# One load for wo and one for w1, two more w2 blocks as column products, and a bf16 turn of the result

## The chip, the cores and the metric

The kernel runs on one core of one Trainium2 chip. The metric is the device time of an execution in microseconds (us); each time below is the median of several executions, with the range. A profile shows a slightly shorter *span*, from the first to the last instruction: in most executions here 1.3 us less than the time. All executions named below count as fast: none is more than 1.5% above the fastest of the same kernel. The engines are PE (tensor; PEld is its weight load), DVE (vector), ACT (scalar), POOL (GpSimd) and SP, whose queue issues all loads. Sixteen DMA engines carry the data.

## The reference

One decode step of a conditioned transformer block, two sequences, one new token each. Cut to what matters:

```python
mod = (silu(c) @ w_mod)                       # six shift, scale and gate vectors
h = layernorm(x) * (1 + ca) + sa
q = h @ wq                                    # 32 heads of 128
p = softmax(q @ k_cache.T / sqrt(128))        # 4 kv heads, 32768 keys: 8 pairs (batch, kv head)
x = x + ga * ((p @ v_cache) @ wo)             # wo: 4096 x 1024, 8.4 MB
h = layernorm(x) * (1 + cb) + sb
z = gelu(layernorm(h) @ w1 + b1)              # w1: 1024 x 3584, 7.3 MB
x = x + gb * (z @ w2 + b2)                    # w2: 3584 x 1024, 7.3 MB
```

Two rows of work against 178 MB of weights and cache: the kernel mostly reads.

## The kernel before

All loads go through one ring of 160 KB per partition, in a fixed order: w_mod, wq, then for each of the eight pairs two K halves (slots at 0 and 32 KB) and V (slot at 64 KB), then wo, w1, w2. A load is issued as soon as what lay in its place has been used; `frees` makes the queue wait for that.

```python
for m, off in enumerate((128, 0)):
    add(("wo", m), [16, DM], A_wo[m * 2048:(m + 1) * 2048, :].rearrange("(p j) n -> p j n", j=16), off * KB)
for m, off in enumerate((32, 64)):
    add(("w1", m), [4, F], w1_v[:, 4 * m:4 * m + 4, :], off * KB)
W2_ITEMS = ((0, 8, 96), (8, 16, 112), (16, 24, 128), (24, 27, 144), (27, 28, 150))   # blocks j0..j1 at KB
```

The output layers come in two shapes. A *row product* holds the activations still (128x32) and streams 512 weight columns past them; four of them fill the four column groups of the array, and the sums lie in rows that must be turned into columns afterwards (`load_row`, a DVE copy, then `to_columns`, four products with a small selection matrix). A *column product* holds 128x128 weights still and streams two activations; its sums are columns at once.

```python
for m in range(2):                       # wo: 2 x 32 row products into one bank
    it = need("wo", m)
    for j in range(16):
        for hf in range(2):
            ...matmul(psS[0][32 * q:32 * q + 32, :], lhsT=atT[m][:, j, :], rhs=w[:, j, hf * 512:(hf + 1) * 512])
load_row("dve", psS[0], "psS0", 0)
to_columns(psM, "psM", 0, True, True)
# ... residual, two layernorms, then w1: 8 x 8 row products, transpose, gelu -> gT ...
for g in range(16):                      # w2, first 16 blocks: row products
    ...
load_row("dve", psS[0], "psS0", 3)
to_columns(psO, "psO", 3, True, False)
for g in range(16, FT):                  # w2, last 12 blocks: 8 column products each, added on top
    ...
mT = psO * mod(5); res_bf = mT + x1b     # two DVE operations
matmul(psM[0:16, 0:128], lhsT=res_bf, rhs=ident)     # turn to 16 rows of 128, fp32 PSUM
res16 = copy(psM[0:16, 0:128])
```

## Time and profile before

| | |
|---|---|
| time | 420.07 us, 3 executions, 420.02 to 420.12 |
| span of the profiled execution | 418.7 us |
| DMA queue busy, share of the span | 98.8% |
| PE, DVE, ACT busy | 70%, 50%, 36% |
| bytes read from HBM | 178.28 MB, 426 GB/s over the span |

Two lines of the page: from part 1 the busy time of each engine, and from part 6 the issue of wo (count, size of each, median us from issue to landing).

```profile
PE 291.0 (70%) x5183; PEld 231.3 (55%) x5183; DVE 209.6 (50%) x423; ACT 149.4 (36%) x179; POOL 6.8 (2%) x29
...
wo<-in_A_wo_dram SPq DMA_DIRECT2D x2, 4096.0 KB, 39.0
```

No compute engine is busy for the whole span. A 4 MB load takes about 9.7 us by itself at 430 GB/s but lands 39 us after its issue: some 30 us of other loads stand ahead of it. That backlog is what a change of issue times eats into.

### The profile page before, as it was taken

To read this page: it belongs to the slowest core of one execution; us is meant where nothing else is said; L and a number is where in the kernel's file an instruction comes from. 1 tells how busy PE (TensorE), PEld (TensorE's weight loads), DVE (VectorE), ACT (ScalarE), POOL (GpSimd) and SP (SyncE) were. 2 spreads that over 40 slices of the span, in tenths; PEclk is the share of its full clock that TensorE was granted. 3 is DMA by queue.
4 is the path that set the end of the run, shared out by engine and by line. 5 is a ranking of instruction groups with operands and counts; after the bars stand their busy time and mean duration, and the time that the engine had idled before them with its cause. 6 is when DMAs were issued, how large, how long until landed. Compare 5 with 4: busy or idle time off the path is not lost.

```text
span 418.7 us, 11609 instructions
## 1 busy us (share of the span) xinstructions
PE 291.0 (70%) x5183; PEld 231.3 (55%) x5183; DVE 209.6 (50%) x423; ACT 149.4 (36%) x179; POOL 6.8 (2%) x29
## 2 busy tenths in 40 slices
PE   1407449766996895699369957976995699564536
PEld 1104219762993794299149926962894399221214
DVE  1201105546677676467726664766477567620411
ACT  2000015533565364256405632643365166400100
POOL 3000000000000000000000000000000000000000
PEclk9999557986896997799589958986697889576585
DMA  9989999999999999999999999999999999899995
GB/s 373 450 380 449 448 404 493 398 406 446 441 432 429 423 451 429 419 454 457 391 435 476 407 416 448 438 438 426 438 438 426 416 460 457 377 448 428 424 427 249
DMA packets 5581, 178.42 MB, mean 426 GB/s; under 512 B 698, under 2 KB 706, under 8 KB 964
## 3 DMA queue, kind: packets, MB, share of 16 engines
q1 hardware_dynamic: 5572, 178.28, 98.8%
q8 instruction: 8, 0.13, 0.1%
q14 instruction: 1, 0.01, 0.0%
HBM read 178.28 MB, written 0.00 MB: 426 GB/s over the span
## 4 chain that ended last, share of the span: by engine, by line
DMA 71%; PE 24%; DVE 2%; issue 1%; ACT 1%; SPq 1%
DMA V<-in_A_v_cache_dram 39%; DMA wo<-in_A_wo_dram 10%; DMA K<-in_A_k_cache_dram 10%; PE psZ L584 10%; DMA w<-in_B_w_dram 9%; PE psKT L536 8%; DMA wmod<-in_w_mod_dram 4%; PE psS L548 1%; PE psZ L548 1%; PE psS L655 1%; PE psZ L729 1%; PE psZ L469 1%; ACT KT_sb L540 0%; PE psS L469 0%; DVE m1c L553 0%
## 5 line engine op out<-in xcount | busy, mean ns | idle before, releaser
L536 PE MATMUL psKT<-ident,K 128*128 128x128 bf16 x2048 | 163.1, 229 | 11.5 <-DMA K<-in_A_k_cache_dram 11.5
L540 ACT ACTIVATE KT_sb<-psKT 128x1024 bf16<-128x1024 bf16 x96 | 98.2, 1025 | 124.4 <-PE psKT L536 124.4
L542 DVE COPY KT_sb<-psKT 128x1024 bf16<-128x1024 bf16 x160 | 106.7, 688 | 61.6 <-PE psKT L536 61.2
L536 PEld LDWEIGHTS psKT<-ident,K 128*128 128x128 bf16 x2048 | 126.7, 102 | 13.0 <-DMA K<-in_A_k_cache_dram 12.7
L584 PE MATMUL psZ<-V,E_sb 128*32 128x512 bf16 x512 | 46.4, 541 | 23.2 <-DMA V<-in_A_v_cache_dram 20.0
L548 PE MATMUL psS<-qcur,KT_sb 128*128 128x8 bf16 x1024 | 44.7, 167 | 2.2 <-issue 2.2
L584 PEld LDWEIGHTS psZ<-V,E_sb 128*32 128x32 bf16 x512 | 18.7, 130 | 47.7 <-issue 38.8
L548 PE MATMUL psZ<-qcur,KT_sb 128*128 128x8 bf16 x1024 | 43.0, 167 | 2.2 <-issue 1.5
L548 PEld LDWEIGHTS psS<-qcur,KT_sb 128*128 128x128 bf16 x1024 | 40.0, 97 | 2.3 <-issue 2.3
L548 PEld LDWEIGHTS psZ<-qcur,KT_sb 128*128 128x128 bf16 x1024 | 37.9, 96 | 3.4 <-issue 1.6
L572 ACT ACTIVATE E_sb<-S_sb 128x512 bf16<-128x512 f32 x32 | 19.5, 630 | 29.6 <-DVE S_sb L570 29.6
L570 DVE TENSOR_TENSOR S_sb<-S_sb,gmb 128x512 f32<-128x512 f32 x32 | 20.0, 685 | 0.3
L576 DVE TENSOR_REDUCE rs<-E_sb 128x8 f32<-128x512 bf16 x32 | 19.7, 675 | 0.0
L469 PE MATMUL psS<-wmod,inT 128*32 128x512 bf16 x32 | 5.1, 624 | 16.2 <-DMA wmod<-in_w_mod_dram 16.2
L553 DVE TENSOR_REDUCE m1c<-psZ 128x8 f32<-128x512 f32 x16 | 11.1, 693 | 10.2 <-ACT S_sb L552 10.1
L595 DVE RECIPROCAL rinv<-psM 128x1 f32<-128x1 f32 x8 | 1.3, 168 | 27.7 <-PE psM L593 27.7
L605 PE MATMUL psM<-msum,hmat 128*128 128x128 f32 x16 | 4.2, 347 | 13.3 <-DVE msum L600 13.3
L559 PE MATMUL psM<-identf,m 128*8 128x128 f32 x16 | 4.3, 369 | 13.1 <-DVE m L556 13.1
L553 DVE TENSOR_REDUCE m1c<-psS 128x8 f32<-128x512 f32 x16 | 11.1, 693 | 3.2 <-ACT S_sb L552 3.1
L552 ACT ACTIVATE S_sb<-psZ 128x512 f32<-128x512 f32 x16 | 9.5, 595 | 7.5 <-PE psZ L548 7.5
L477 DVE COPY S_sb<-psS 128x512 f32<-128x512 f32 x1 | 0.7, 690 | 22.9 <-PE psS L469 22.9
L469 PEld LDWEIGHTS psS<-wmod,inT 128*32 128x32 bf16 x32 | 1.1, 132 | 19.3 <-DMA wmod<-in_w_mod_dram 18.0
(123 smaller groups left out, 167.5 us busy)
## 6 DMA issues: line engine op xcount, KB each, us to landing
K<-in_A_k_cache_dram SPq DMA_DIRECT2D x16, 4096.0 KB, 27.1
wq<-in_A_wq_dram SPq DMA_DIRECT2D x2, 4096.0 KB, 44.8
wo<-in_A_wo_dram SPq DMA_DIRECT2D x2, 4096.0 KB, 39.0
w<-in_B_w_dram SPq DMA_DIRECT2D x2, 3584.0 KB, 32.5
wmod<-in_w_mod_dram SPq DMA_DIRECT2D x1, 6144.0 KB, 29.8
w<-in_B_w_dram SPq DMA_DIRECT2D x3, 2048.0 KB, 37.8
wmod<-in_w_mod_dram SPq DMA_DIRECT2D x1, 4608.0 KB, 15.8
wmod<-in_w_mod_dram SPq DMA_DIRECT2D x1, 1536.0 KB, 6.0
```

Of the source, the lines that this page charges most:

```text
L469: pe(lambda e, w=it.view, k=k, kk=kk, ch=ch, n=n, q=q: e.matmul(bank[n][32 * q:32 * q + 32, :], lhsT=inT[:, k, :], rhs=w[:, kk, ch * 512:( ...
L536: pe(lambda e, kq=kq, jj=jj, w=kt, t=t: e.transpose(psKT[kq][:, jj * 128:(jj + 1) * 128], w[:, t, :], ident[:, :]), reads=[it.reg, "ident" ...
L540: act(lambda e, src=src: e.activation(KT_sb[g8][:, :, :], src, ACT.Copy), reads=[f"psKT{kq}"], writes=[f"KT_sb{g8}"], sem=f"ev{cc}_{g8}")
L542: dve(lambda e, src=src: e.tensor_copy(KT_sb[g8][:, :, :], src), reads=[f"psKT{kq}"], writes=[f"KT_sb{g8}"], sem=f"ev{cc}_{g8}")
L548: pe(lambda e, t=t, jj=jj: e.matmul(ps[:, t * HPG:(t + 1) * HPG], lhsT=KT_sb[g8][:, jj, :], rhs=qcur[:, :], start=True, stop=True), reads= ...
L552: act(lambda e: e.activation(Sc, ps.rearrange("p (t h) -> p h t", h=HPG), ACT.Copy), reads=[preg], writes=[f"S_sb_{cc}"], sem=f"sc{cc}")
L553: dve(lambda e: e.tensor_reduce(m1c[:, :, cc], ps.rearrange("p (t h) -> p h t", h=HPG), AX.X, ALU.max), reads=[preg], writes=[f"m1c{cc}"])
L559: pe(lambda e: e.matmul(psM[0:HPG, 0:128], lhsT=m1[:, :], rhs=identf[:, :], start=True, stop=True), reads=["m1", "identf"], writes=["psM"])
L570: dve(lambda e: e.tensor_tensor(Sc, Sc, gmb[:, :].unsqueeze(2).to_broadcast([128, HPG, TPC]), ALU.subtract), reads=[f"S_sb_{cc}", "gmb"], ...
L572: act(lambda e: e.activation(Ec, Sc.rearrange("p h (u t) -> p u h t", t=4), ACT.Exp, scale=SCALE), reads=[f"S_sb_{cc}"], writes=[f"E_sb_{c ...
L576: dve(lambda e: e.tensor_reduce(rs4[:, :, cc], Ec.rearrange("p u h t -> p h u t"), AX.XY, ALU.add), reads=[f"E_sb_{cc}"], writes=[f"rs4_{c ...
L584: pe(lambda e, t4=t4, tg=tg, q=q: e.matmul(psO[32 * q:32 * q + 32, :], lhsT=E_sb[:, tg // 4, :, :].rearrange("p h t -> p (h t)"), rhs=vt[: ...
```

## The change

Its intent: fewer and larger loads for the two output layers of the attention and the feed-forward part, less row work just ahead of the last loads, and a cheaper end. Wo becomes one load with 64 KB in a row for each partition, w1 one load with 56 KB. The ring places move accordingly. The attention result is laid out for the new order of wo's rows (other shapes of the same small operations in the loop). Blocks 14 and 15 of w2 go from row to column products and run beside the row copy. The result is turned by a transpose into a bf16 PSUM tile. The core of the diff:

```diff
-W2_ITEMS = ((0, 8, 96), (8, 16, 112), (16, 24, 128), (24, 27, 144), (27, 28, 150))
+W2_ITEMS = ((0, 8, 64), (8, 16, 80), (16, 24, 0), (24, 27, 16), (27, 28, 22))
+W2_ROWS = 14
...
-    for m, off in enumerate((128, 0)):
-        add(("wo", m), [16, DM], A_wo[m * 2048:(m + 1) * 2048, :].rearrange("(p j) n -> p j n", j=16), off * KB)
-    w1_v = B_w1.rearrange("(p k) n -> p k n", k=KT8)
-    for m, off in enumerate((32, 64)):
-        add(("w1", m), [4, F], w1_v[:, 4 * m:4 * m + 4, :], off * KB)
+    add(("wo", 0), [32, DM], A_wo.rearrange("(p j) n -> p j n", j=32), 0)
+    add(("w1", 0), [8, F], B_w1.rearrange("(p k) n -> p k n", k=KT8), 104 * KB)
...
-    for g in range(16):
+    for g in range(W2_ROWS):
...
     load_row("dve", psS[0], "psS0", 3)
-    to_columns(psO, "psO", 3, True, False)
+    for g in range(W2_ROWS, 16):
+        w2_columns(g, g == W2_ROWS)
+    to_columns(psO, "psO", 3, False, False)
...
-    pe(lambda e: e.matmul(psM[0:16, 0:128], lhsT=res_bf..., rhs=ident[:, :], start=True, stop=True), ...)
-    dve(lambda e: e.tensor_copy(res16[:, :], psM[0:16, 0:128]), ...)
+    pe(lambda e: e.transpose(psKT[0][0:16, 0:128], res_bf..., ident[:, :]), ...)
+    dve(lambda e: e.tensor_copy(res16[:, :], psKT[0][0:16, 0:128]), ...)
```

## The prediction

> **What bounds the kernel now.** I read the page first (engine shares, slices, queues), then the chain that ended last in order of time, then the timeline of the last 80 us, because every part of the change acts after 330 us except three loop operations of the same size. From the page:
>
> ```profile
> DMA  9989999999999999999999999999999999899995
> ...
> q1 hardware_dynamic: 5572, 178.28, 98.8%
> ...
> DMA 71%; PE 24%; DVE 2%; issue 1%; ACT 1%; SPq 1%
> ```
>
> The first row is the busy share of the 16 DMA engines in 40 slices: it is full from the second slice to the last but one. The second says that the packets of the load queue fill 98.8% of the span, 0.988 x 418.7 = 413.7 us. So no more than 5 us of the span are free of transfers, and they lie at the two ends: about 2 us until the first load runs, and about 3 us after the last one. The chain (third row) agrees. A change in compute is worth nothing unless it shortens that last stretch. The tail of the chain, as start, length and what:
>
> ```profile
> 330.98 41.08 DMA wo<-in_A_wo_dram
> 372.10 3.28 PE psS L655 x32
> 375.40 37.83 DMA w<-in_B_w_dram
> 413.27 1.87 PE psZ L729 x64
> 415.17 1.03 PE psZ L729 x32
> 416.22 0.19 DVE mT L732
> 416.43 0.24 DVE res_bf L733
> 416.72 0.29 PE psM L734
> 417.03 0.28 DVE c L736
> ```
>
> Read it as one stream of loads that lasts until the third w2 item is in (413.27), then 96 small products back to back, then two vector operations, the turn, a copy and the store. Between 372 and 413 the tensor engine does all of the two output layers inside the waits for loads. The timeline shows how much room is there (start, length, engine, what, and in brackets the idle time and its releaser):
>
> ```profile
> 355.02 21.65 SPq L389 DMA_DIRECT2D w<-in_B_w_dram  x7
> 372.10 3.25 PE L655 MATMUL psS<-wo,atT 128*32 128x512 bf16 x32 [0.78 <-DMA wo<-in_A_wo_dram]
> 381.73 3.55 PE L655 MATMUL psS<-wo,atT 128*32 128x512 bf16 x32 [6.39 <-DMA wo<-in_A_wo_dram]
> 385.34 0.69 DVE L664 COPY S_sb<-psS 128x512 f32<-128x512 f32 x1 [13.23 <-PE psS L655]
> 395.75 1.68 PE L696 MATMUL psZ<-w,inT 128*32 128x448 bf16 x16
> 398.74 1.35 PEld L696 LDWEIGHTS psZ<-w,inT 128*32 128x32 bf16 x32 [0.38 <-DMA w<-in_B_w_dram]
> 400.59 1.12 DVE L704 STREAM_TRANSPOSE S_sb<-psZ 128x896 f32<-128x896 f32 x1 [2.84 <-PE psZ L696]
> 403.68 1.05 PE L720 MATMUL psS<-w,gT 128*32 128x512 bf16 x16 [3.15 <-DMA w<-in_B_w_dram]
> 408.41 1.90 PE L720 MATMUL psS<-w,gT 128*32 128x512 bf16 x16 [3.69 <-DMA w<-in_B_w_dram]
> 411.11 1.87 PE L668 MATMUL psZ<-half,S_sb 128*128 128x4 f32 x8 [0.80 <-DVE S_sb L664]
> ```
>
> The loads' landings can be read off the waits that they end: wo halves 372.1 and 381.7, second half of w1 398.7, w2 items 403.7, 408.4 and 413.27. The row-shaped part of w2 ends at 411.11 + 1.87 = 412.98, only 0.3 us ahead of the landing that it must beat. That 0.3 us is the narrow place.
>
> **What the Trainium skill says.** "DMA: Bandwidth & Descriptors", Specifications, gives 435 GB/s as the ceiling of the path into SBUF. The trace agrees that nothing is left: the second wo half, 4.194 MB, landed 381.73 - 372.10 = 9.63 us after the first, 435 GB/s; w1 and three w2 items, 13.63 MB, took 413.27 - 381.73 = 31.54 us, 432 GB/s. The same page, "Queues, rings and completion order", says each DMA engine consumes its ring's descriptors in order; the trace fits, since landings follow the issue order. So a load that is issued early enough loses nothing by being issued later. "TensorE: Matmul & The Clock Gate", Part 1, gives half clock until about 3.4 us of sustained work. The trace shows it: the first half of wo took 3.25 us at a granted clock near 0.5, about 107 ns a product, while 32 products of w1 after 398.74 took 1.79 us, 56 ns each. "VectorE: DVE Perf Modes", "Why PSUM operands drop a tier", says an fp32 PSUM operand runs at 1x and that 2x_1P is the most any PSUM operand gets. In the trace the fp32 copy of 512 columns took 690 ns and the bf16 copy of 1024 columns 688 ns, so bf16 from PSUM does go twice as fast here.
>
> **The change, part by part.**
>
> Wo in one load, placed at 0 to 64 KB. Before, the first half went to a free slot and was issued at 330.98. Now the load needs both K slots, and the second is free when its last transposes end: 355.02, when the first w1 load is issued today. The queue still holds the last V load then; its products start at 362.51. So 7.5 us of backlog remain, and no gap opens. The w1 load now needs the V slot, free at about 368.8 (products start 362.51 and take 6.34), with wo still running to 381.7: 12.9 us of backlog. The third w2 item waits for wo's products, at worst 388.2 (381.7 + 6.5), with w1 and two w2 items queued until 408.4. No gap either.
>
> Larger packets. The trace's records of single packets (no view prints them) give medians of 1213 ns for 32 KB, 2418 ns for 64 KB and 1062 ns for 28 KB. Wo: 16 engines carry 256 packets of 32 KB, 16 each, 19.41 us; in 64 KB packets 8 x 2.418 = 19.34. That is 0.06 us less. For w1 at 56 KB I take the same relative gain, 0.33% of 17 us, 0.06 us. Two loads fewer save two completions, perhaps 0.03 us. Sum 0.13 to 0.15 us, and it does reach the end: every later landing moves forward.
>
> Later start of wo's products. They now all wait for 381.6. The attention product has the same shape and count, 64 of 128x512, and took 5.2 to 6.5 us by the chain (6.34 in its last round, cold). Starting cold and warming after 3.4 us gives 3.4 + 32 x 0.054 = 5.2; so 386.9 to 388.1, against 385.3 now: 1.6 to 2.8 us later, all of it in compute. From the row copy to the first w1 product today is 395.75 - 385.34 = 10.41 us, so the input of w1 is ready at 397.3 to 398.5. W1's single load lands at 398.6. So the delay vanishes into that wait.
>
> W1 in one load. 64 products of 448 columns start at 398.6, where 32 were done by then before. Cold they take 94 ns (448 columns at the cold rate above), warm about 50 to 56. All cold: 6.0 us, to 404.6; warming after 3.4 us: 36 cold, 28 warm, 4.9 us, to 403.5. Today the transpose starts at 400.59. So this costs 2.9 to 4.0 us. The transpose, gelu and product with it need 403.68 - 400.59 minus the wait, which is 2.15 us (400.59 to 402.74), so w2's input is ready at 405.7 to 406.8.
>
> W2. Its first item landed at 403.6: 16 products of 1.05 to 1.75 us end at 406.8 to 408.5. The second lands at 408.3. Now 12 row products follow instead of 16: 12/16 of about 1.75 + 0.15 us of drain gives 1.45, to 409.8 or 410.0. The row copy of 0.69 us follows, and beside it on the tensor engine run the 16 column products of blocks 14 and 15, 16 x 29 ns = 0.46 us (29 ns from 2.91 us for 96). They are hidden in the copy. Turning the row takes 1.87 cold: 412.4 to 412.6. This is ahead of 413.1, the new landing of the third item; the margin is 0.5 to 0.7 us instead of 0.3. So the two extra column blocks buy 0.4 us in the narrow place, which only serves as room.
>
> The tail. 96 column products as before. The turn of the result stays one instruction of about 0.28 us. Its copy reads 128 columns of bf16 instead of fp32: from 690 ns for 512 fp32 columns and 278 for 128, a column costs 1.07 ns and the fixed part is 140; at half a column's cost it is 140 + 69 = 209. Gain 0.07 us.
>
> Sum: -0.14 in the stream, -0.07 in the tail, the compute delay hidden: 420.07 - 0.21 = 419.86.
>
> **The rivals.** First, the compute chain no longer fits: if wo's and w1's products both fall badly in the clock windows, or a product takes longer with all weights in one stage, the row turn ends after 413.1 and every excess goes to the end one for one. The cold sums put the end at 412.6 at the latest, so I expect at most 0 to 0.8 us of loss, up to 420.7. The 0.3 us of margin today speak for it, the four fewer row products against it. Second, a gap in the load stream: if 7.5 us of backlog at 355 are not enough because the later issue finds engines that drained early, there would be a wait of up to 1 to 2 us before wo. The landings of the attention loop, where V is issued with one or two loads queued ahead and the row of slices stays full, speak against it. It would make 421 to 422. Third, larger packets may do nothing, and only the tail counts: 420.0. Fourth, a warm clock at the end would shorten the 96 column products, but only to the last landing, which is near 415.8; at most 0.2 us, 419.6.
>
> **Range and chances.** Mostly a sum of tenths, so a narrow range: 419.3 if packets and clock both help and the chip is a little faster, 420.7 if the first rival is at work. A change of 2% would need 8.4 us, more than the span that is free of transfers, so faster by 2% can be ruled out: 0.005. Slower by 2% would need a gap that no backlog above allows: 0.015.
>
> **What would show it.** Right: load queue share still near 98.8%; wo's 64 products start near 381.6 and w1's 64 near 398.6, both after a wait for their load; the transpose of w1's sums at 403.5 to 404.6; the row turn ending before the wait for the third w2 item, near 413.1; the final copy near 0.21 us. Wrong: an idle stretch of the DMA row around 343 to 365, a row turn that directly precedes the last column products without a wait for a load, or landings of wo and w1 that moved by more than 0.5 us.

## The result, and the profile after

| | before | changed |
|---|---|---|
| time, same rounds | 420.14 us (420.02 to 420.28, 6 executions) | 420.32 us (419.88 to 421.27, 6 executions) |
| the same again, other rounds | 420.00 us (419.92 to 420.23, 9) | 420.10 us (419.79 to 420.31, 5) |
| span of the profiled execution | 418.7 us | 418.6 us |

The ratio is 1.0006 in the first rounds (95% interval 0.9993 to 1.0019) and 1.0000 in the second (0.9987 to 1.0014). A ratio is the mean time of one kernel's fast runs over that of the other's of the same rounds, so not quite the ratio of the medians quoted. The change made no measurable difference.

The page after, the same three rows as the prediction shows of before: DMA share by slice, load queue, chain by engine.

```profile
DMA  9989999999999999999899999999999999999996
...
q1 hardware_dynamic: 5284, 178.28, 98.8%
...
DMA 65%; PE 32%; DVE 1%; issue 1%; ACT 0%; SPq 0%
```

The queue has 288 packets fewer (5572 - 5284) and is as full as before. The third row looks like a shift from DMA to PE, but it is not one in the stage of the change: the chain only takes another way through the attention loop, where PE's release of a K slot and the load that follows are followed back in turn. The tail of the chain shows what ends the kernel (start, us, what):

```profile
354.93 26.79 DMA wo<-in_A_wo_dram
...
381.76 6.55 PE psS L652 x49
...
388.33 24.90 DMA w<-in_B_w_dram
...
413.27 2.86 PE psZ L716 x96
...
416.65 0.29 PE psKT L736
...
416.96 0.21 DVE c L737
```

Wo is issued at 354.93 instead of 330.98 and 344.68 (its halves), and its last part is in at the same time as before (381.76 against 381.73). The 96 column products start at 413.27 in both kernels, to the hundredth. The last copy took 0.21 us instead of 0.28. Between these, the timeline (start, length, engine, what, and the idle time before with its releaser):

```profile
381.76 6.51 PE L652 MATMUL psS<-wo,atT 128*32 128x512 bf16 x64 [10.67 <-DMA wo<-in_A_wo_dram]
388.33 0.69 DVE L661 COPY S_sb<-psS 128x512 f32<-128x512 f32 x1 [16.45 <-PE psS L652]
398.76 0.17 PEld L693 LDWEIGHTS psZ<-w,inT 128*32 128x32 bf16 x8 [0.73 <-DVE inT L497]
405.07 1.12 DVE L701 STREAM_TRANSPOSE S_sb<-psZ 128x896 f32<-128x896 f32 x1 [4.27 <-PE psZ L693]
407.27 2.60 PE L725 MATMUL psS<-w,gT 128*32 128x512 bf16 x28 [2.26 <-DVE gT L708]
408.40 0.14 PEld L725 LDWEIGHTS psS<-w,gT 128*32 128x32 bf16 x8 [0.58 <-DMA w<-in_B_w_dram]
409.93 0.69 DVE L661 COPY S_sb<-psS 128x512 f32<-128x512 f32 x1 [2.42 <-PE psS L725]
410.68 1.87 PE L665 MATMUL psZ<-half,S_sb 128*128 128x4 f32 x8 [0.28 <-DVE S_sb L661]
413.27 2.85 PE L716 MATMUL psZ<-gT,w 128*128 128x2 bf16 x96 [0.73 <-DMA w<-in_B_w_dram]
```

Read it against the same rows in the prediction. Every compute step up to the row products of w2 is later: wo's row copy 388.33 against 385.34, w1's transpose 405.07 against 400.59, w2's first row products 407.27 against 403.68. The row products of the first w2 item now wait for gT, made by DVE, and no longer for their load. The 2.60 us of the 28 are two stretches: the weight loads of the second item, at 408.40, still waited for theirs, and began when they had before (408.41). So the later start is gone there. The row copy after 12 instead of 16 products of that item starts at 409.93 instead of 410.36, the row turn ends at 410.68 + 1.87 = 412.55 instead of 412.98, and the last row waits 0.73 us for its load.

### The profile page after: what moved, and what is told of

Read it like the earlier page. It is cut to its first block, busy times and chain, and to the rows that moved or that the text cites. A ratio compares the mean times of both kernels' runs of the same rounds, so it can differ in the third digit from the quotient of the medians.

```text
span 418.6 us, 11630 instructions
## 1 busy us (share of the span) xinstructions
PE 294.4 (70%) x5195; PEld 235.5 (56%) x5195; DVE 209.7 (50%) x423; ACT 149.4 (36%) x179; POOL 7.3 (2%) x28
## 3 DMA queue, kind: packets, MB, share of 16 engines
q1 hardware_dynamic: 5284, 178.28, 98.8%
## 4 chain that ended last, share of the span: by engine, by line
DMA 65%; PE 32%; DVE 1%; issue 1%; ACT 0%; SPq 0%
DMA K<-in_A_k_cache_dram 49%; PE psKT L534 21%; DMA wo<-in_A_wo_dram 6%; DMA w<-in_B_w_dram 6%; DMA wmod<-in_w_mod_dram 4%; PE psS L546 4%; PE psZ L546 2%; PE psS L652 2%; PE psZ L582 1%; PE psZ L716 1%; PE psZ L467 1%; PE psS L467 0%; DVE msum L598 0%; DVE m1c L551 0%; DVE KT_sb L540 0%
## 5 line engine op out<-in xcount | busy, mean ns | idle before, releaser
L534 PE MATMUL psKT<-ident,K 128*128 128x128 bf16 x2048 | 165.1, 230 | 11.5 <-DMA K<-in_A_k_cache_dram 11.5
L534 PEld LDWEIGHTS psKT<-ident,K 128*128 128x128 bf16 x2048 | 128.6, 103 | 13.1 <-DMA K<-in_A_k_cache_dram 13.0
L582 PE MATMUL psZ<-V,E_sb 128*32 128x512 bf16 x512 | 46.8, 546 | 23.2 <-DMA V<-in_A_v_cache_dram 21.5
L652 PE MATMUL psS<-wo,atT 128*32 128x512 bf16 x64 | 6.5, 596 | 10.7 <-DMA wo<-in_A_wo_dram 10.7
```

The source lines that it names most:

```text
L534: pe(lambda e, kq=kq, jj=jj, w=kt, t=t: e.transpose(psKT[kq][:, jj * 128:(jj + 1) * 128], w[:, t, :], ident[:, :]), reads=[it.reg, "ident" ...
L582: pe(lambda e, t4=t4, tg=tg, q=q: e.matmul(psO[32 * q:32 * q + 32, :], lhsT=E_sb[:, tg // 4, :, :].rearrange("p h t -> p (h t)"), rhs=vt[: ...
L652: pe(lambda e, w=it.view, j=j, hf=hf, q=q: e.matmul(psS[0][32 * q:32 * q + 32, :], lhsT=atT[:, j, :], rhs=w[:, j, hf * 512:(hf + 1) * 512] ...
```

## The experiments

Theory: the stream of loads sets the end, the whole change lies beside it, and the single loads have used up room in the compute chain. Rivals: compute spills over in some runs; larger packets shorten the stream; the later issue opens a gap.

### Changed kernel again

No edit; on the same chip and in the same rounds as the next three.

> The changed kernel unaltered, to have it on the same chip as the next three. Theory (the load stream sets the end, all compute of the change is hidden): 420.0 us, a ratio to before between 0.999 and 1.001, profiled span 418.6 +- 0.2. Rival (compute after wo no longer fits in some runs, as a 421.27 us run with a span of 420.0 suggests): some runs 0.5 to 1.5 us longer than the shortest, a wider spread than before has.

It gave 420.10 us (419.79 to 420.31), spans of 418.5 to 418.9. The wider spread of the first rounds did not come back. Two of those six executions had 2.0 us outside a normal span of 418.6, and one, of 421.27 us, had a span of 420.0. No trace of that one was kept.

### The w2 part undone

```diff
-W2_ROWS = 14
+W2_ROWS = 16
-        w2_columns(g, g == W2_ROWS)
-    to_columns(psO, "psO", 3, False, False)
+        w2_columns(g, False)
+    to_columns(psO, "psO", 3, True, False)
```

> The changed kernel with the w2 part undone: 16 blocks of w2 as row products again, none more as columns. Theory: the row turn ends about 0.4 us later than in the changed kernel (412.55), near 413.0, still just ahead of the third w2 item (413.27); time the same as the changed kernel within 0.2 us. Rival (the two column blocks are needed to hold the time): the turn ends after 413.3 and the time rises by 0.2 to 0.5 us.

It gave 419.85 us (419.82 to 419.88), ratio 0.9996 (0.9982 to 1.0009). The row turn ended at 412.05, not near 413.0: the turn itself ran at full clock, in 1.05 us instead of 1.87. So 16 row blocks also fit.

> The changed kernel with 16 row blocks again, a second time: the first gave 419.82 to 419.88 where the changed kernel gave 419.79 to 420.31. If undoing the w2 part is worth 0.2 us: 419.8 to 419.9 again with the narrow spread. If that was a good draw: 419.8 to 420.3.

419.97 us (419.88 to 419.98), beside 420.02 of before. Both intervals contain 1 (the second ratio is 0.9997, 0.9983 to 1.001). The two extra column blocks neither pay nor cost anything that these runs can tell.

### Both loads in two again

```diff
-    add(("wo", 0), [32, DM], A_wo.rearrange("(p j) n -> p j n", j=32), 0)
+    for m in range(2):
+        add(("wo", m), [16, DM], wo_v[:, 16 * m:16 * m + 16, :], 32 * m * KB)
-    add(("w1", 0), [8, F], B_w1.rearrange("(p k) n -> p k n", k=KT8), 104 * KB)
+    for m, off in enumerate((104, 132)):
+        add(("w1", m), [4, F], w1_v[:, 4 * m:4 * m + 4, :], off * KB)
```

> The changed kernel with wo and w1 each in two loads again (halves of a partition's 64 and 56 KB), the rest as changed. Theory: same landings within 0.1 us, time the same within 0.2 us; wo's products end near 385.3 instead of 388.3 and w1's sums are turned near 400.6 instead of 405.1, so the compute has 3 to 4 us more room, which the time does not show. Rival (larger packets or fewer loads shorten the stream): 0.1 to 0.2 us slower than the changed kernel and landings later by that. Rival (compute spills in some runs of the changed kernel): narrower spread than the changed kernel, and 0.1 to 0.5 us faster on average.

It gave 421.00 us (420.09 to 421.31), ratio 1.002 (1.0006 to 1.0034), the slowest of its rounds. But its spans were 418.5 to 418.7, as short as the others'. The excess lay outside the profiled span, 1.4 to 2.6 us there instead of 1.3. In the profile the copy of wo's rows started at 385.28 and w1's transpose at 401.82, about 3 us earlier than in the changed kernel; the weight loads of w2's second item stood idle for 3.73 us until it landed, against 0.58 in the changed kernel and 4.18 in the kernel before; and the last products started at 413.43. Is the excess a property of the kernel?

> The changed kernel with wo and w1 in two loads each, a second time: the first gave 420.09 to 421.31 with spans of 418.5 to 418.7, that is, 1.4 to 2.6 us outside the profiled span where other kernels have 1.3. If that belongs to the kernel: 420.6 to 421.3 again in most runs. If it belonged to those executions: 420.0 to 420.3 and 1.3 us outside the span.

420.16 us (419.98 to 420.36), 1.3 to 1.6 us outside the span. So the excess belonged to those executions. What it was stays open. The room moved by 3 us and the end did not, as the theory says, and it is the single loads that take the room. What fewer loads bring, no time shows; the section on why has what the landings show.

### A known delay, in both kernels

Sixty-four further products of wo's shape ahead of the real ones, written to a bank that is overwritten later; the result stays right. In the changed kernel they stand ahead of all of wo, in the kernel before ahead of its second half.

```diff
     it = need("wo", 0)
+    for x in range(64):
+        pe(... matmul(psS[1][32 * (x % 4):32 * (x % 4) + 32, :], lhsT=atT[:, 0, :], rhs=w[:, 0, 0:512], start=True, stop=True) ...)
```

> The changed kernel with 64 further products of the same shape ahead of wo's 64, into a bank that is overwritten later (the result stays right): a known delay of 3 to 4 us in the compute between wo and w2, no more bytes. Theory (the single loads moved the room from before w1 to after w2's rows, and about 0.7 to 1.5 us of it is left): the third w2 item still lands near 413.3, but the row turn ends after it, and the time rises by 1.3 to 3.0 us, to 421.5 to 423. Rival (all compute is hidden with ample room as in the kernel before): no change, 420.0 to 420.3.

> The kernel before with the same 64 further products ahead of the second half of wo, into the same bank. Theory (before, the compute chain waits some 3.7 us for the second w2 item, so a delay upstream is absorbed there): w2's first row products start 3 us later, the time stays within 0.3 us of the kernel before. Rival (the delay adds to the end): 2 to 4 us slower, as in the run before this one.

| | time | before, same rounds | ratio |
|---|---|---|---|
| changed kernel with the delay | 422.12 us (421.63 to 422.17) | 420.10 us | 1.0044 (1.0027 to 1.0060) |
| kernel before with the delay | 420.15 us (420.06 to 420.21) | 420.10 us | 1.0001 (0.9984 to 1.0018) |

The timeline of the changed kernel with the delay, from w1's transpose on:

```profile
408.36 1.12 DVE L706 STREAM_TRANSPOSE S_sb<-psZ 128x896 f32<-128x896 f32 x1 [4.06 <-PE psZ L698]
...
413.99 1.87 PE L670 MATMUL psZ<-half,S_sb 128*128 128x4 f32 x8 [0.27 <-DVE S_sb L666]
415.72 2.70 PE L721 MATMUL psZ<-gT,w 128*128 128x2 bf16 x96
```

And of the kernel before with it:

```profile
405.12 1.12 DVE L710 STREAM_TRANSPOSE S_sb<-psZ 128x896 f32<-128x896 f32 x1 [3.15 <-PE psZ L702]
...
410.40 1.05 PE L674 MATMUL psZ<-half,S_sb 128*128 128x4 f32 x8 [0.80 <-DVE S_sb L670]
413.42 2.87 PE L735 MATMUL psZ<-gT,w 128*128 128x2 bf16 x96 [1.96 <-DMA w<-in_B_w_dram]
```

In the first, the transpose is 3.3 us later than without the delay (408.36 against 405.07), the row turn ends at 415.86, and the column products follow it without any wait for a load. The time rises by 2.0 us. In the second, the transpose is 4.5 us later (405.12 against 400.59), and the column products still wait 1.96 us for their load. This is the main thing that the change did to the kernel, and its time does not show it. Before, compute between wo and w2 could be 4.5 us slower for nothing; now a delay of 3.3 us costs 2.0.

### Wo issued after V has landed

Wo takes V's place in the ring, w1 the K places; the queue then issues wo only when the last attention product is done.

```diff
-    add(("wo", 0), ..., 0)
-    add(("w1", 0), ..., 104 * KB)
+    add(("wo", 0), ..., 64 * KB)
+    add(("w1", 0), ..., 0)
-W2_ITEMS = ((0, 8, 64), (8, 16, 80), (16, 24, 0), (24, 27, 16), (27, 28, 22))
+W2_ITEMS = ((0, 8, 128), (8, 16, 144), (16, 24, 64), (24, 27, 80), (27, 28, 86))
```

> The changed kernel with wo placed on V's slot instead of K's two slots (w1 takes the K slots, w2 the free ones): wo is issued only when the last attention product is done, near 368.5, while the last V load landed at 362.4. Theory (the stream is full only as long as a load is issued before the one ahead has landed; the changed kernel has 7.5 us of that): the DMA engines stand idle from 362.4 to the issue plus about 1.9 us (the first load of the kernel took that from issue to data), 8.0 us, and the time rises by 7.5 to 8.5 us, to 427.5 to 428.5. Rival (the move of the issue is hidden by other transfers or the compute sets the end): under 2 us.

It gave 429.92 us (429.16 to 430.40), ratio 1.0230 (1.0213 to 1.0248). The DMA row of its page and its issue of wo, from the timeline:

```profile
DMA  9999999999999999999999999999999995599895
...
368.80 0.35 SPq L387 DMA_DIRECT2D wo<-in_A_wo_dram  x1
...
390.67 5.84 PE L652 MATMUL psS<-wo,atT 128*32 128x512 bf16 x64 [19.45 <-DMA wo<-in_A_wo_dram]
```

The two fives are the gap. Wo landed at 390.67 instead of 381.76, 8.9 us later, of which 6.4 are the later issue (368.80 against V's landing at 362.4) and 2.5 the way from issue to data (390.67 - 368.80, less eight packets of 2.418 us). I had taken 1.9 for the latter. A further 1.2 us came between wo and the third w2 item, which is told below. So the changed kernel's wait for both K slots is safe only because the last V load is still running then.

### Small packets for wo

```diff
-    add(("wo", 0), [32, DM], A_wo.rearrange("(p j) n -> p j n", j=32), 0)
+    add(("wo", 0), [32, DM], A_wo.rearrange("(j p) n -> p j n", j=32), 0)
```

> The changed kernel with wo's rows dealt to the partitions one by one, so that its load is 4096 packets of 2 KB instead of 128 of 64 KB (the result is wrong on purpose: the rows no longer fit the stationary operand). Theory (the stream costs the sum of its packets' times, 84 ns for 2 KB and 2418 ns for 64 KB, and every microsecond of it reaches the end): 256 x 84 ns = 21.5 us against 19.3, so all later landings and the time move by 2.2 us, to 422.2. Rival (packet overheads are hidden, so that the size of packets does not count, and the 0.13 us that the prediction gave to larger packets is nothing): within 0.3 us of the changed kernel.

It gave 421.45 us (421.00 to 421.77), ratio 1.0033 (1.0016 to 1.0050). Wrong rows meet the stationary operand, as intended; the comparison still passed, so it is not sharp enough to see this part. The load queue of its page, and the wait that wo's landing ended:

```profile
q1 hardware_dynamic: 9252, 178.28, 99.0%
...
382.83 5.20 PE L652 MATMUL psS<-wo,atT 128*32 128x512 bf16 x64 [12.78 <-DMA wo<-in_A_wo_dram]
```

With 3968 packets more (9252 - 5284) wo landed 1.07 us later (382.83 against 381.76), half of the 2.2 expected, and the end moved by about as much: the spans are 419.7 to 419.9, against 418.6 to 419.0 for the kernel before in the same rounds and 418.5 to 418.9 for the changed kernel in others. The median rose by more, 1.35 us, but two of the four executions had 1.9 us outside the span. So whatever lengthens the stream does reach the end. But the records of single packets cannot simply be added: 256 packets of 84 ns per engine are 21.5 us, and the load took about 20.4, the changed kernel's 19.35 plus 1.07. The records of small packets overlap.

### Two attempts to beat both

After the last load there remain column products, two DVE operations, the turn, the copy and the store. In both attempts the residual is turned early into an fp32 PSUM tile (in a wait) and the last product is accumulated on it by its own turn, so that one DVE operation goes.

```diff
+    matmul(psM[0:16, 0:128], lhsT=x1r, rhs=identf, start=True, stop=False)        # early
-    mT = psO * mod(5); res_bf = mT + x1b; transpose(psKT[0][0:16, 0:128], res_bf, ident)
+    mR = psO * mod(5)                                                             # bf16
+    matmul(psM[0:16, 0:128], lhsT=mR, rhs=ident, start=False, stop=True)
```

The first attempt stands on the kernel with both loads in two:

> An attempt to beat both: loads in two as in the run before, and the last addition taken off the end: the residual with its bias term is turned early into the fp32 PSUM tile, and the last product's turn is accumulated on it, so that one vector operation (0.24 us) and its hand-over go, while the last copy reads fp32 again (+0.07 us). Theory (everything after the last load counts one for one): 0.15 to 0.2 us off the stretch from the last column product to the store (1.07 us in the changed kernel), time near 419.8. If the end were bound elsewhere: no difference.

420.09 us (419.79 to 420.26), no gain. The store was issued at 417.04 instead of 417.20, but landed at 418.70. Its instruction queue and its store (size, us from issue to landing), from the page's DMA parts:

```profile
q8 instruction: 9, 0.15, 0.1%
...
out_dram<-c SPq DMA_DIRECT2D x1, 4.0 KB, 1.6
```

Before and after have eight such fetches and 1.4 for the store. The ninth ran at 416.4 for 1.29 us. Of the store's 16 landings, 15 came by 418.39 and one at 418.67. The second attempt stands on the changed kernel's loads and 16 row blocks, with fewer instructions:

> Second attempt to beat both: the changed kernel's single loads, w2 with 16 row blocks again, and the residual accumulated into the turn as in the first attempt. In the first attempt the store was issued 0.14 us earlier than in the changed kernel but landed 1.66 us after its issue instead of 1.41; its trace has a ninth instruction fetch of 16 KB, at 416.4 us and 1.29 us long, beside the store. This version has fewer instructions than the first attempt and about as many as the run with 16 row blocks, which had eight fetches and none there. Theory (the fetch held back the store): eight fetches, store landing 1.2 to 1.4 us after its issue, span 418.3 to 418.4, time 419.7. Rival (the store lands when the stream's last load plus about 2.9 us is over, whatever its issue): span 418.5 to 418.7, as all others.

```profile
q8 instruction: 8, 0.13, 0.1%
...
out_dram<-c SPq DMA_DIRECT2D x1, 4.0 KB, 1.3
```

Eight fetches; all 16 landings of the store between 418.23 and 418.39. The time was 419.86 us (419.59 to 419.99) beside 420.02 of before, ratio 0.9994 (0.9981 to 1.0008); spans 418.3 to 418.7. It holds the lowest single time, 419.59, and the profiled stretch is shorter as predicted. But the interval contains 1, so it is not shown to be faster.

### More instruction fetches

Semaphore increments that nobody waits for, 400 to 700 to an engine, ahead of wq's products and of the attention loop.

```diff
+    for _ in range(700):
+        T.raw("pool", lambda e: e.sem_inc(dummy["pool"], 1))     # likewise pe 400, act 700, dve 600
```

> The changed kernel with 2400 semaphore increments that nobody waits for, on tensor, scalar, vector and GpSimd engines in their idle time before the attention loop: about nine more instruction fetches of 16 KB, no other work and no more loads. Theory (a fetch holds its one DMA engine back by about 1.2 us for good, a load has landed when its last engine has, and the fetches go round the engines: 8 of 16 are late at the end today): with 17 or more fetches some engine is hit twice and all later landings move by about 1.2 us, time 421.2 to 421.5. Rival (fetches fill gaps of the stream): time as the changed kernel, 420.0 to 420.3, and the spread of the 16 landings of a load as it was, 1.6 us.

462.19 us (461.15 to 463.28): as a timing, a failed experiment. PE stood still from 46.3 to 92.1 us with its 300 increments, some 0.15 us each, and loads waited for it, so that the stream had holes of about 40 us. It made only two further fetches of 16 KB (ten), but 18 of 8 KB on another queue instead of one. Its time tells nothing about the question.

The first part of its trace does, for the stream was full until 70 us (DMA share 0.98 to 1.04 between 40 and 70). Each of a load's 16 engines has a landing record, which no view prints. After one 8 KB fetch (at 10.41) one engine landed the second w_mod load at 18.19, 0.48 us behind the other 15; after three (the last at 31.08) one landed the third at 33.99, 1.80 us behind the rest, where in the changed kernel all 16 came between 31.74 and 32.12. The second wq load was complete at 54.63 instead of 52.65. So an engine falls behind with fetches, falls further behind with more of them, and holds up the whole load. What that costs at the end of a kernel without holes is not shown: after the first hole the spread of K and V landings fell from 4.2 us to 1.5.

## Why the prediction was right, and which terms were off

*What bounds the kernel.* Right. The load queue stayed at 98.8%, and the stretch from the third w2 item to the store was what remained after it. The experiments say so from the other side: 1.07 us more of load moved the end by about as much, and a gap with what followed it moved it by 9.8.

*No gap from the later issue.* Right in direction and size: wo's wait ended at 381.76 against 381.73. The experiment that issued it 13.9 us later still (368.80 against 354.93) opened the gap that the rival had described. It was larger than the 1 to 2 us of the rival and than the 8 of the expectation.

*Larger packets, 0.13 to 0.15 us.* The gain is in the stream, smaller than forecast; that it reaches the end is the step that no run bears out. The engines of one load do not land together. From V's landing to that of the third w2 item, the first engine to land took 50.85 to 50.87 us in six profiles with single loads (this kernel twice, 16 row blocks twice, the delay, the second attempt) and 50.91 to 50.99 in five with loads in two (before, before with the delay, both loads in two twice, the first attempt): 0.09 us less on average. But the products wait for the last engine, and there it took 50.81 to 51.17 and 50.86 to 51.11. A scatter of 0.3 us hides the gain. The 0.03 us for two completions had no source in a trace. Adding the records of single packets came out near enough here, and twice too large for 2 KB packets.

*Wo's products, done at 386.9 to 388.1.* Done at 388.3, just outside. I let the clock rise 3.4 us after the start. The same page of the Trainium skill ("TensorE: Matmul & The Clock Gate", Part 1) also says that the window is free-running and does not start with the work, which I left out. The trace agrees: its clock records, which no view prints, change at 387.63, 391.05, 404.70 and 408.11, whole steps of 3.41 us. So here the clock became full 5.9 us after wo's first product, with 2 KB packets 3.2 us after it, and in the other runs with wo in one load 4.1 to 5.4. (The sum has a slip too: 3.4 + 32 x 0.054 is 5.1, not 5.2.)

*W1's start hidden at 398.6.* Right, by a hair: its products start at 398.76, and the wait before them is for the layernorm's result and no longer for the load. That is where the 3 us of room before this point had gone (before, the first products started at 395.75 and the second half of w1 came at 398.74).

*W1's products, transpose at 403.5 to 404.6.* It came at 405.07, and at 404.62 and 404.64 in two other runs. The same error with the clock: the products ran at the half rate until 404.70.

*W2's row turn done at 412.4 to 412.6.* 412.55, and by the way forecast. The 16 products of the first item started 3.6 us late (407.27 against 403.68) at full clock, the last of them at 407.94, and the second item's could start only when it had landed, at 408.41 as before: that wait took up the whole delay. Its 12 products ran at the half rate, as the 16 did before, so the row copy came 0.43 us earlier (409.93 against 410.36). The turn was cold, as assumed; at full clock in the repeated run it ended at 411.96. The column products beside the copy took 0.58 us, not 0.46 (2.91 / 96 is 30 ns, not 29), still less than the copy's 0.69. The margin was 0.7 us, as said. The first rival (compute spills) did not happen at this margin, and the run with the delay shows that it does with 3.3 us more.

*The tail, 0.07 us.* The copy took 0.21 us instead of 0.28, as worked out, but no time shows it. The runs cannot resolve 0.07 us: the spans of one kernel vary by 0.1 to 0.4.

*The sum, 419.86.* Measured 420.32 and 420.10. Nothing of the forecast 0.21 us could be seen in the time. About 0.09 of the 0.14 is there in the first landings and 0.07 in the length of the copy, but the scatter of the last landing, and of the time, is larger than both. That the time lay inside a range of 1.4 us says little about either term.

What stays open: what the extra 0.6 to 1.3 us outside the span of some executions was, and why one execution of the changed kernel had a span of 420.0. The last section has a guess for the latter; no trace of that execution was kept. A small case of it: in the second profile of this kernel one engine ran 0.46 us behind all others from w1 on, and the last products started at 413.50 instead of 413.27.

## What to carry to other kernels

Where a stream of loads is full from end to end, count what a change does to bytes, gaps and the stretch after the last load; all else only moves room about. Moving room is still an effect: a merged load makes its consumer start later and all at once, and a delay that cost nothing before then costs time, which an added known delay in both kernels shows and the plain times do not. Merge loads when the chain behind them has room, and check how long the backlog is at the moment of the later issue.

## What the Trainium skill lacked or had wrong

- "Runtime: NRT & Kernel Launch", Instruction fetch mechanics, calls the cost of crossing a 16 KiB boundary mostly hidden, and no page that I read says that instruction fetches hold up the load stream. Here each of the eight 16 KB fetches is followed by one more of the 16 engines running behind. The landing records of the changed kernel, which no view prints, in us:

```text
last w_mod load, before the first fetch:   all 16 between 31.74 and 32.12
first wq load, after the fetch at 36.3:    15 between 41.42 and 41.76, one at 42.97
last w2 load, after eight fetches:         7 between 414.07 and 414.35, one at 414.88, 8 between 415.27 and 415.67
```

  The one between the groups first appears after the only 8 KB fetch (at 82.34). In the run with the gap all 16 landings of wo fell between 390.18 and 390.63, so the gap had let the late engines catch up. After its next fetch (396.4) 15 of w1's lay between 407.13 and 407.53 and one at 408.82, 1.3 us behind; this is the further 1.2 us of that run. A load has landed when its last engine has. That fetches cause the lag is inferred from these times and from the first 55 us of the run with more of them; its end does not test it. An engine hit twice would explain the one span of 420.0 us; that is a guess.
- "DMA: Bandwidth & Descriptors", Anatomy of one DMA, gives about 2.0 us of fixed cost for another issue path. From the queue used here, the run with the gap shows 2.5 us from the issue of wo until its data had landed, less the time of its packets.
- The same page's Bandwidth section, under Why small descriptors are slow, gives about 3 cycles of overhead for a packet, with one example of 256 bytes and none in a full stream. By it a 2 KB packet, 64 beats of 32 bytes, would be some 4.7% slower, as an estimate. Here 2 KB packets instead of 64 KB made an 8.4 MB load 1.07 us slower, about 5.5%.
- I found no page with the cost of a semaphore increment as an instruction of its own: on PE 300 of them took 46 us, about 0.15 us each.
